# The first strip's third weight group by seven products, with six raw places and a copy pool that opens later

## The chip, the cores and the metric

The kernel runs on one core of a Trainium2 chip. The metric is device time in microseconds. Before the change it was 868.43 us, the median of three runs (868.04 to 869.34).

Five engines work side by side, each through its own list of instructions in order: TensorE (PE) for matmuls, which write to PSUM; VectorE (DVE); ScalarE (ACT); GpSimd (POOL); and SyncE (SP), which here only issues transfers. Semaphores carry the dependences between them.

## The reference

Linear attention for 8 batches of 8 heads, 576 positions and 64 features, followed by a feed-forward block over the 4608 tokens:

```python
kv  = einsum('bhsd,bhse->bhde', k, v)
out = einsum('bhsd,bhde->bhse', q, kv)
x   = out / sqrt(mean(out * out) + 1e-6) * g_norm     # (4608, 512) after the heads are joined
h   = x @ w_in                                        # 512 -> 2048
y   = relu(h) ** 2 @ w_out                            # 2048 -> 512
```

The weights arrive as 64-bit floats and are converted on the chip.

## The kernel before

**Strips.** The 4608 tokens are nine strips of 512. Each strip goes through two products: "up" (x times w_in, with the squared ReLU) and "down" (times w_out). Strip 0 is computed while its weights still arrive. Its up product runs as 16 plain steps (`up_first`, L900 to L918): four groups of the hidden features, four steps in a group, each step eight matmul instructions with 512 columns. After each step ACT makes a ReLU in PSUM (L916) and two squares into the `gt` tiles (L918). Four PSUM places (`fpsum`) take the steps in turn.

From strip 1 on, the up product of a group is made by seven half-size products (`up`, with `ORDER` 1, 2, 6, 5, 7, 3, 4). They use three PSUM banks: 1, 6, 7 and 4 add up in one, 5 and 3 in another, 2 has its own. After 1, 6 and 5 ACT copies the bank as a snapshot (`combine`, L880), and later products are added to these. Seven products need four sums of x (`sums_x`) and three sums of the weights (`sums_in`). Strip 0's down product uses the same scheme with weights (`down`).

**Conversion of weights.** A raw weight comes in pieces of 512 KB. Two pieces make a pair, and a pair has one place in `raw_pool` (five places). For each pair ACT makes two copies (L260 into `w_c`, which has two places, and L262 in place), POOL clamps (L282), and DVE joins the bits in two steps (L284, L288). `convert(n)` emits conversions up to the n-th behind the steps of the up product; the list `PACE` says how far after each. When it emits the conversion of pair n it first emits ACT's copies of pair n+1, and then the loads of later pieces (`load_more`), up to `AHEAD` = 10 pieces ahead. Pairs 0 to 7 are w_in; 8 to 15 are w_out. The last four pairs are also summed by DVE in `sums_out` into tiles called `wt`, which take places of `raw_pool` too, and are stored to DRAM from there (L336).

**Order.** All instructions are emitted by hand in one order, and each engine keeps that order. Between the steps `attend` emits the next pieces of the attention: transposes of q (`t_ps`, copied by ACT at L422), key-value products (`kv_ps`, copied by ACT at L453 and L454 into `kv_all`), products with the queries (`x_ps`, L484, which read `kv_all`), squares (L493), means, and scaled rows. SP issues all loads and stores, in order, too.

**Pools.** SBUF is given out as a stack of pools. The pools for the conversion (`xt_pool`, `raw_pool`, `spare_pool`, `wtmp`) lie on top of it; when strip 0's up product is emitted they are closed, and `stream_pool` and `sum_pool` are opened in the same room. A place there may be written only after the work on what lay there has ended. Both are opened with `reuse_waits="tile"`. The pool of snapshots and outputs (`c_pool`, six places) is opened at the start, below the conversion pools, and has its room to itself.

```python
conv = ExitStack()
xt_pool = conv.enter_context(tc.tile_pool(name="xt", bufs=1))
raw_pool = conv.enter_context(tc.tile_pool(name="raw", bufs=5))
...
conv.close()
stream_pool = ctx.enter_context(tc.tile_pool(name="stream", bufs=6, reuse_waits="tile"))
sum_pool = ctx.enter_context(tc.tile_pool(name="sum", bufs=8, reuse_waits="tile"))
```

Of the kernel before, what the change touches and what calls it, by code (L numbers as in the profile page):

```python
# [10 lines left out]
FP32 = mybir.dt.float32  # L11
# [3 lines left out]
AF = mybir.ActivationFunctionType  # L15
ALU = mybir.AluOpType
# [4 lines left out]
def kernel(  # L21
# [34 lines left out]
    nc = tc.nc  # L56
    P = 128
# [13 lines left out]
    TH = STRIP // 2  # L71
# [4 lines left out]
    SQ = 32  # L76
    Q_ON_PE = 2
    BEHIND = 1.6
    X_ON_PE = 2
    EPS = 1e-6  # L80
    AHEAD = 10
    PACE = (3, 4, 4, 5, 6, 7, 8, 9, 10, 11, 12, 13, 13, 14, 15, 16)
    const = ctx.enter_context(tc.tile_pool(name="const", bufs=1))
    wpool = ctx.enter_context(tc.tile_pool(name="wpool", bufs=1))
# [4 lines left out]
    small = ctx.enter_context(tc.tile_pool(name="small", bufs=3))  # L89
    g_pool = ctx.enter_context(tc.tile_pool(name="g", bufs=4))  # L90
    dram = ctx.enter_context(tc.tile_pool(name="dram", bufs=1, space=bass.MemoryType.DRAM))
    c_pool = ctx.enter_context(tc.tile_pool(name="c", bufs=6))
    conv = ExitStack()
    xt_pool = conv.enter_context(tc.tile_pool(name="xt", bufs=1))
    raw_pool = conv.enter_context(tc.tile_pool(name="raw", bufs=5))
    spare_pool = conv.enter_context(tc.tile_pool(name="spare", bufs=1))
    wtmp = conv.enter_context(tc.tile_pool(name="wtmp", bufs=2))
    psums = ExitStack()
    fpsum = psums.enter_context(tc.tile_pool(name="fpsum", bufs=4, space=bass.MemoryType.PSUM))
# [61 lines left out]
    def load_rest(b, eng):  # L161
        h = b % 2 * (b > Q_ON_PE + 1)
        half = slice(REST * h, REST * (h + 1))
        for t, src in ((k_rest[half], k), (v_rest[half], v)):
            eng.dma_start(out=t, in_=src[b, :, C * P : S].rearrange("h s d -> s h d"))
# [20 lines left out]
    def load_next(q_eng=nc.sync, names="kvq"):  # L186
        u = next(to_load, None)
        if u is not None:
            load(*u, q_eng, names)
# [27 lines left out]
    KH, FH, DH = NP // 2, d_ff // 2, d_model // 2  # L217
    FQ = FC // 2
    WN = 512
    NG = FQ // 2  # L220
# [3 lines left out]
    block = lambda b: w_in[:, :, :, b] if b < 4 else w_s[:, :, :, b - 4]  # L224
# [14 lines left out]
    raw = []  # L239
    raw_pairs = []  # L240

    def load_piece():
        i = len(raw)
        if i < len(sources):
            if i % 2 == 0:
                raw_pairs.append(raw_pool.tile([P, 2, 2, WN // 2], I64, name="raw", tag="raw"))
            t = raw_pairs[i // 2][:, i % 2]
            nc.sync.dma_start(out=t, in_=sources[i])
            raw.append(t)
# [42 lines left out]
    def convert_pair(n, dest):  # L292

        for i in range(acted[0], min(n + 2, len(sources) // 2)):
            convert_pair_on_act(i)
            acted[0] = i + 1
        deque(conversion(pair_words.pop(n), dest, nc.gpsimd), 0)
        load_more(2 * n + 2)

    def load_more(end):  # L300

        while len(raw) < min(end + AHEAD, max(len(sources) - 4, end + AHEAD - 4), len(sources)):
            load_piece()

    def minus(eng, out, a, b):
        eng.tensor_tensor(out=out, in0=a, in1=b, op=ALU.subtract)  # L306
# [3 lines left out]
    def pieces_in(i):  # L310
        g, k = divmod(i // 2, KH)
        convert_pair(i // 2, w_in[:, k, g].rearrange("p (a b) e -> p a (b e)", a=2))

    def sums_in(g):

        nc.scalar.activation(w_in[:, :, g, 0:4], w_in[:, :, g, 0:4], AF.Copy, scale=g_col)
        a11, a21, a12, a22, s1, s2, s4 = (block(b)[:, :, g] for b in range(7))
        nc.vector.tensor_tensor(out=s1, in0=a21, in1=a22, op=ALU.add)
        minus(nc.vector, s2, s1, a11)
        minus(nc.vector, s4, a12, s2)  # L320
        minus(nc.vector, a21, a11, a21)
# [24 lines left out]
    def convert(n):  # L346
        while converted[0] < min(n, len(conversions)):
            fn, a = conversions[converted[0]]
            fn(a)
            converted[0] += 1  # L350
# [337 lines left out]
    xc = {}  # L688

    def halves(s, kh, th):  # L690
        return xt[s][:, ts(th, TH // SQ), ts(kh, KH), :]

    def sums_x(s):
        xc[s] = t1, t2, t3, t4 = [
            sum_pool.tile([P, TH // SQ, KH, SQ], FP32, name=f"x_t{i}", tag="sum") for i in range(4)
        ]
        x = lambda kh, th: halves(s, kh, th)
        minus(nc.vector, t1, x(0, 1), x(0, 0))
        minus(nc.vector, t2, x(1, 1), t1)
        minus(nc.vector, t3, x(1, 1), x(0, 1))  # L700
        minus(nc.vector, t4, x(1, 0), t2)
# [99 lines left out]
    def attend_between(slot, begun, goal, late, first, last):  # L801
# [6 lines left out]
        while slice_at[0] < most:  # L808
# [6 lines left out]
            if fn != send_x:  # L815
                left = sum(f != send_x for f, _ in slices[slice_at[0] : goal])
                if used and (on in used or fn in (root, inverse) or used & {root, inverse}):
                    return
                if left <= last - slot and behind[on] + cost > BEHIND:
                    return  # L820
# [28 lines left out]
    ORDER = (1, 2, 6, 5, 7, 3, 4)  # L849
    BANK = {1: "A", 6: "A", 7: "A", 4: "A", 5: "B", 3: "B", 2: "C"}  # L850
    A_IN = {1: 0, 2: 2, 3: 6, 4: 3, 5: 4, 6: 5, 7: 1}
    B_OUT = {1: 0, 2: 1, 5: 2, 7: 3, 3: 4, 6: 5, 4: 6}
    bank, snap, gq, w_blk = {}, {}, {}, {}

    def open_bank(p):
        b = BANK[p]
        if p in (1, 5, 2):
            bank[b] = fpsum.tile([P, 2, 2 * P], FP32, name=f"ps_{b}", tag="f")
        return bank[b]
# [7 lines left out]
    def product(p, i, lhsT, rhs, n):  # L867

        for k in range(n):
            nc.tensor.matmul(  # L870
                bank[BANK[p]][:, i, :], lhsT=lhsT(k), rhs=rhs(k),
                start=p in (1, 5, 2) and i == 0 and k == 0, stop=k == n - 1, skip_group_check=True,
            )

    def combine(p, c11, c12, c21, c22):

        b = bank[BANK[p]]
        if p in (1, 6, 5):
            snap[p] = c_pool.tile([P, 2, 2 * P], FP32, name=f"snap{p}", tag="c")
            nc.scalar.copy(snap[p], b)  # L880
        elif p == 4:
            c21(b)
        else:
            other, c = {2: (1, c11), 7: (5, c22), 3: (6, c12)}[p]
            c(b, snap[other])

    def quarters(s, g):

        if (s, 11) not in gq:
            for q in (11, 12, 21, 22):  # L890
                gq[s, q] = g_pool.tile([P, FQ, TH], FP32, name="gt", tag="gt")
        return {q: gq[s, q][:, 2 * g : 2 * g + 2, :] for q in (11, 12, 21, 22)}
# [27 lines left out]
    def up(s, g, p):  # L920
        open_bank(p)
        rhs = {
            1: halves(s, 0, 0), 2: halves(s, 1, 0), 3: halves(s, 1, 1),
            4: xc[s][3], 5: xc[s][0], 6: xc[s][1], 7: xc[s][2],
        }[p]
        for i in range(2):
            product(p, i, lambda kc: block(A_IN[p])[:, kc, g, ts(i, P)], lambda kc: rhs[:, :, kc, :], KH)
        dest = quarters(s, g)

        def relu_squared(q):  # L930
            def f(b, a):
                o = dest[q]
                nc.vector.tensor_tensor(out=o, in0=b, in1=a, op=ALU.add)
                nc.vector.scalar_tensor_tensor(out=o, in0=o, scalar=0.0, in1=o, op0=ALU.max, op1=ALU.mult)
            return f

        def last(b):
            nc.scalar.activation(dest[21], b, AF.Relu)
            nc.scalar.activation(dest[21], dest[21], AF.Square)

        combine(p, relu_squared(11), relu_squared(12), last, relu_squared(22))
# [66 lines left out]
    def down(s, p, i):  # L1008
# [27 lines left out]
        def store(th, eh):  # L1036
# [7 lines left out]
            return f  # L1044

        combine(p, store(0, 0), store(0, 1), store(1, 0), store(1, 1))


# [310 lines left out]
    for s in range(N_STRIP):  # L1359
# [7 lines left out]
        if s >= DEEP_UP:  # L1367
            steps = [(0.5, up_slot, (s, slot)) for slot in range(55)]
        elif s == 0:
            steps = [(2, up_first, (g, fh, i)) for g in range(NG) for fh in range(2) for i in range(2)]  # L1370
        else:
            steps = [(1, up, (s, g, p)) for g in range(NG) for p in ORDER]
        n_up = len(steps)
# [9 lines left out]
                goal = min(pair_ends, key=lambda end: abs(end - goal))  # L1383
        total, done = sum(w for w, _, _ in steps), 0
        for i, (w, fn, a) in enumerate(steps):
            if s == 0 and i < n_up:

                if i == 0:
                    load_next()
                    load_rest(1, nc.sync)  # L1390
                    load_next()
                if i == 1:
                    load_next()
                if i == 2:
                    for b in range(2):
                        load_q_rest(b, nc.sync)
                if i == 14:
                    for b in range(2):
                        store_first(b)
            elif s == 0 and i == n_up:  # L1400
                convert(len(conversions))
                conv.close()

                stream_pool = ctx.enter_context(tc.tile_pool(name="stream", bufs=6, reuse_waits="tile"))
                sum_pool = ctx.enter_context(tc.tile_pool(name="sum", bufs=8, reuse_waits="tile"))
            if s == 0 and n_up <= i < n_up + 2:
# [5 lines left out]
            fn(*a)  # L1412
            if s == 0 and i < n_up:

                convert(PACE[i])
            done += w
            if s:
                clock[0] += 3.2 if i >= n_up else 2.2 if s == DEEP else 1.2
                soon = tiles_due and tiles_due[0][2][0] // NT == s + 1
                if i == n_up + 10:  # L1420
                    while tiles_due and tiles_due[0][2][0] // NT == s + 1:
                        _, f, a = tiles_due.popleft()
# [35 lines left out]
                sums_in((7, 8, 9, 12).index(i - n_up))  # L1458
            if i == n_up + 11:
                sums_x(1)  # L1460
            n = i + 1 - (n_up - 6)
            pairs, m = divmod(max(n - 2 * NP, 0), 3)
            attend(min(ready[0] + min(max(n, 0), 2 * NP) + (n >= 2 * NP) + 4 * pairs + (0, 2, 2)[m], goal))
            while deep_due and i not in (n_up + 1, n_up + 4, n_up + 12, n_up + 13):
# [38 lines left out]
```

## Time and profile before

| what | value |
|---|---|
| median of three runs | 868.43 us |
| the profiled execution | 868.8 us, of which the span of its instructions is 867.0 |
| PE busy | 857.8 us, 99% of the span |
| DVE busy | 702.0 us, 81% |
| ACT busy | 348.9 us, 40% |
| POOL busy | 328.1 us, 38% |
| strip 0's up steps on PE | up to 82.3 us |
| strip 0's down product on PE | from 83.1 to 138.2 us |

Times in the profile are counted from the start of the span. A row of a timeline gives the start, the duration, the engine, the line of the kernel, the operation, the tiles it writes and reads, its shape, and how many instructions are merged; in brackets stands the idle time before it and what ended that. Matmuls overlap, so the time that one takes on the engine is the distance to the next one's start, not its duration. A row of the lines' view gives minimum, median and maximum duration in ns. Shares of busy time are means over stages with different limits.

### The profile page before, as it was taken

To read this page: it belongs to the slowest core of one execution; us is meant where nothing else is said; L and a number is where in the kernel's file an instruction comes from. 1 tells how busy PE (TensorE), PEld (TensorE's weight loads), DVE (VectorE), ACT (ScalarE), POOL (GpSimd) and SP (SyncE) were. 2 spreads that over 40 slices of the span, in tenths; PEclk is the share of its full clock that TensorE was granted. 3 is DMA by queue.
4 is the path that set the end of the run, shared out by engine and by line. 5 is a ranking of instruction groups with operands and counts; after the bars stand their busy time and mean duration, and the time that the engine had idled before them with its cause. 6 is when DMAs were issued, how large, how long until landed. Compare 5 with 4: busy or idle time off the path is not lost.

```text
span 867.0 us, 32426 instructions
## 1 busy us (share of the span) xinstructions
PE 857.8 (99%) x14176; PEld 804.2 (93%) x14176; DVE 702.0 (81%) x1132; ACT 348.9 (40%) x777; POOL 328.1 (38%) x335
## 2 busy tenths in 40 slices
PE   7999999999999999999999999999999999999998
PEld 6445888889999999999999999999999999999998
DVE  3768988879877996789688967897889777975887
ACT  4888241320048303750356034901491148102810
POOL 1223004630458223730574045704470447145700
PEclk9999999999999999999999999999999999999999
DMA  9898998999999997989698979987678856885583
GB/s 307 277 362 269 274 377 239 295 332 353 280 264 259 342 325 233 228 307 344 209 244 273 341 239 281 283 297 270 198 236 302 301 165 221 293 282 196 175 315 121
DMA packets 169469, 236.46 MB, mean 273 GB/s; under 512 B 78704, under 2 KB 133744, under 8 KB 161008
## 3 DMA queue, kind: packets, MB, share of 16 engines
q1 hardware_dynamic: 169024, 234.33, 83.5%
q8 instruction: 111, 1.82, 0.9%
q14 instruction: 30, 0.25, 0.1%
q10 hardware_dynamic: 304, 0.07, 0.0%
HBM read 197.66 MB, written 36.70 MB: 270 GB/s over the span
## 4 chain that ended last, share of the span: by engine, by line
PE 83%; DMA 7%; DVE 5%; ACT 3%; SPq 1%; issue 1%; DVEq 0%; ACTq 0%
PE ps_A L865 36%; PE ps_B L865 31%; PE ps_C L865 5%; PE ps_A L870 4%; DMA raw<-in_moe_w_in_dram 2%; PE kv_ps L448 2%; PE x_ps L484 2%; PE ps_B L870 2%; DVE w_t L306 1%; DMA w_deep<-w_t 1%; DMA raw<-in_moe_w_out_dram 1%; DMA w_blk<-w_deep 1%; PE ps_C L870 1%; DMA first_qkv<-in_v_dram 1%; ACT w_c L260 1%
## 5 line engine op out<-in xcount | busy, mean ns | idle before, releaser
L865 PE MATMUL ps_B<-w_blk,g_s 128*64 128x128 f32 x2016 | 122.0, 273 | 0.0
L865 PEld LDWEIGHTS ps_B<-w_blk,g_s 128*64 128x64 f32 x2016 | 112.6, 137 | 0.1
L306 POOL TENSOR_TENSOR x_l<-xT 128x256 f32<-128x256 f32 x21 | 16.2, 773 | 230.2 <-PE ps_A L865 230.2
L865 PE MATMUL ps_B<-w_blk,gt 128*64 128x128 f32 x1504 | 94.1, 273 | 0.3 <-DMA w_blk<-w_deep 0.3
L865 PE MATMUL ps_A<-w_blk,g_s 128*64 128x128 f32 x1536 | 92.2, 273 | 0.0
L1323 POOL TENSOR_TENSOR snap<-snap,gt 128x512 f32<-128x512 f32 x35 | 46.2, 1320 | 112.5 <-ACT snap L1328 93.6
L865 PEld LDWEIGHTS ps_A<-w_blk,g_s 128*64 128x64 f32 x1536 | 85.7, 137 | 0.0
L865 PEld LDWEIGHTS ps_B<-w_blk,gt 128*64 128x64 f32 x1504 | 84.6, 137 | 0.8 <-PE ps_B L865 0.5
L1328 ACT COPY snap<-ps_A 128x512 f32<-128x512 f32 x63 | 36.8, 585 | 103.6 <-PE ps_A L865 96.2
L1263 ACT ACTIVATE gt<-gt 128x512 f32<-128x512 f32 x112 | 70.2, 627 | 9.9 <-DVE gt L1323 9.9
L1264 ACT ACTIVATE gt<-gt 128x512 f32<-128x512 f32 x112 | 70.7, 631 | 3.5
L865 PE MATMUL ps_A<-w_blk,gt 128*64 128x128 f32 x1152 | 71.2, 273 | 0.0
L865 PEld LDWEIGHTS ps_A<-w_blk,gt 128*64 128x64 f32 x1152 | 64.7, 137 | 0.0
L1112 ACT COPY o_sb<-ps_A 128x128 f32<-128x128 f32 x24 | 6.4, 265 | 144.7 <-PE ps_A L865 109.4
L306 DVE TENSOR_TENSOR gt<-gt 128x2048 f32<-128x2048 f32 (+1 forms) x29 | 59.7, 2063 | 0.0
L1111 DVE TENSOR_TENSOR o_sb<-o_sb,ps_B 128x256 f32<-128x256 f32 (+1 forms) x123 | 47.4, 386 | 14.3 <-ACT o_sb L1112 9.5
L865 PE MATMUL ps_A<-x_l,w_in 128*64 128x128 f32 x896 | 58.6, 273 | 0.2 <-DVE gt L1323 0.2
L1323 POOL TENSOR_TENSOR gt<-gt,snap 128x512 f32<-128x512 f32 x42 | 52.5, 1279 | 15.1 <-DVE snap L1323 15.1
L865 PEld LDWEIGHTS ps_A<-x_l,w_in 128*64 128x64 f32 x896 | 50.8, 137 | 0.5 <-DVE gt L1323 0.5
L865 PE MATMUL ps_B<-x_l,w_blk 128*64 128x128 f32 x784 | 51.2, 273 | 0.0
L865 PE MATMUL ps_A<-x_l,w_blk 128*64 128x128 f32 x784 | 51.2, 273 | 0.0
L1112 ACT COPY o_sb<-ps_B 128x128 f32<-128x128 f32 x31 | 8.2, 265 | 96.3 <-PE ps_B L865 96.3
(214 smaller groups left out, 1900.2 us busy)
## 6 DMA issues: line engine op xcount, KB each, us to landing
w_blk<-w_deep SPq DMA_DIRECT2D x56, 1024.0 KB, 7.3
w_blk<-w_out SPq DMA_DIRECT2D x56, 768.0 KB, 6.2
w_blk<-w_in_deep SPq DMA_DIRECT2D x49, 768.0 KB, 5.8
raw<-in_moe_w_in_dram SPq DMA_DIRECT2D x16, 512.0 KB, 9.2
raw<-in_moe_w_out_dram SPq DMA_DIRECT2D x16, 512.0 KB, 8.0
k<-in_k_dram SPq DMA_DIRECT2D x29, 256.0 KB, 4.9
v<-in_v_dram SPq DMA_DIRECT2D x29, 256.0 KB, 5.2
x_d<-x_q SPq DMA_DIRECT2D x27, 256.0 KB, 4.8
```

Source lines behind the costliest of these rows:

```text
L260: nc.scalar.activation(c, high_f, AF.Copy, scale=EXPONENT)
L306: eng.tensor_tensor(out=out, in0=a, in1=b, op=ALU.subtract)
L448: nc.tensor.matmul(ps[ts(h, D), i], lhsT=a, rhs=w, start=i == 0 and c == 0, stop=c == C, skip_group_check=True)
L484: nc.tensor.matmul(ps[half, r, i, ts(p, D)], lhsT=q[row, half], rhs=kvd[b, p][row, row], start=True, stop=True)
L865: nc.tensor.matmul(ps[half], lhsT=lhsT[:, half], rhs=rhs, start=start, stop=stop, skip_group_check=True)
L870: nc.tensor.matmul(bank[BANK[p]][:, i, :], lhsT=lhsT(k), rhs=rhs(k), start=p in (1, 5, 2) and i == 0 and k == 0, stop=k == n - 1, skip_gro ...
L1111: add = lambda out, a, b: nc.vector.tensor_tensor(out=out, in0=a, in1=b, op=ALU.add)
L1112: yield nc.scalar.copy(q[:, 3:4], small(1))
L1263: nc.scalar.activation(o, o, AF.Relu)
L1264: nc.scalar.activation(o, o, AF.Square)
L1323: add = lambda eng, out, a, b: eng.tensor_tensor(out=out, in0=a, in1=b, op=ALU.add)
L1328: nc.scalar.copy(t, ps)
```

## The change

Group 2 of strip 0's up product (`HALVED = 2`) is made by seven products with `up`, in place of four plain steps. Strip 0 has therefore 19 up steps. What belongs to it:

- The list `TURN` maps the new steps to the old turns, so conversions of group 2 are emitted behind the steps 9, 11, 13 and 14 of the list, which are products 2, 5, 3 and 4. The first product has none of its own.
- The sums of strip 0's x are written into the `gt` places of group 3 behind step 3, and the weights' sums (`first_sums_in`) into those of group 2 behind step 5. Both are on DVE.
- The additions of a quarter are on DVE; the squared ReLU of one of them (12) is on ACT.
- The later weight sums of group 2 for the other strips (`sums_in`) take three DVE instructions instead of four.
- The raw pool has six places instead of five, and `AHEAD` is 12 instead of 10.
- `c_pool` is opened after the conversion pools are closed, ahead of `stream_pool`. Until then a pool of its own, `snap_pool` with three places, takes the snapshots of group 2; it belongs to the conversion pools.

```diff
+    HALVED = 2
+    TURN = (*range(8), 7, 8, 8, 9, 9, 10, 11, *range(12, 16))
-    AHEAD = 10
+    AHEAD = 12
-    c_pool = ctx.enter_context(tc.tile_pool(name="c", bufs=6))
-    raw_pool = conv.enter_context(tc.tile_pool(name="raw", bufs=5))
+    raw_pool = conv.enter_context(tc.tile_pool(name="raw", bufs=6))
+    snap_pool = conv.enter_context(tc.tile_pool(name="snap", bufs=3))
...
+    def first_sums_in(g):
+        a11, a21, a12, a22 = (block(b)[:, :, g] for b in range(4))
+        dest = quarters(0, g)
+        first_w[:] = s1, s2, s4 = [dest[q] for q in (22, 12, 21)]
+        nc.vector.tensor_tensor(out=s1, in0=a21, in1=a22, op=ALU.add)
+        minus(nc.vector, s2, s1, a11)
+        minus(nc.vector, s4, a12, s2)
+        minus(nc.vector, a21, a11, a21)
...
     def sums_in(g):
+        if g == HALVED:
+            minus(nc.vector, s2, a22, a21)
+            nc.vector.tensor_tensor(out=s1, in0=s2, in1=a11, op=ALU.add)
+            minus(nc.vector, s4, a12, s2)
+            return
...
     def sums_x(s):
+        else:
+            free = quarters(0, HALVED + 1)
+            ts_x = [
+                free[q].rearrange("p i t -> p (i t)").rearrange("p (a k t) -> p a k t", k=KH, t=SQ) for q in free
+            ]
...
         if p in (1, 6, 5):
-            snap[p] = c_pool.tile([P, 2, 2 * P], FP32, name=f"snap{p}", tag="c")
+            pool, tag = (snap_pool, "snap") if snap_pool else (c_pool, "c")
+            snap[p] = pool.tile([P, 2, 2 * P], FP32, name=f"snap{p}", tag=tag)
...
+            w = first_w[b - 4] if s == 0 and b > 3 else block(b)[:, :, g]
...
+                if s == 0 and q == 12:
+                    nc.scalar.activation(o, o, AF.Relu)
+                    nc.scalar.activation(o, o, AF.Square)
+                    return
...
+                if g == HALVED:
+                    steps += [(1, up, (s, g, p)) for p in ORDER]
...
             elif s == 0 and i == n_up:
                 convert(len(conversions))
                 conv.close()
+                snap_pool = None
+                c_pool = ctx.enter_context(tc.tile_pool(name="c", bufs=6))
                 stream_pool = ctx.enter_context(tc.tile_pool(name="stream", bufs=6, reuse_waits="tile"))
...
-                convert(PACE[i])
+                if i == 3:
+                    sums_x(0)
+                if i == 5:
+                    first_sums_in(HALVED)
+                convert(PACE[turn])
```

## The prediction, made before the change was run

> **What bounds the kernel now.** I read the page first, then TensorE's timeline over the first strip, then ScalarE's and the DMA queue's over the same stretch, then the list of waits.
>
> The page's first part (engine, busy us and share of the span):
>
> ```profile
> PE 857.8 (99%) x14176; PEld 804.2 (93%) x14176; DVE 702.0 (81%) x1132; ACT 348.9 (40%) x777; POOL 328.1 (38%) x335
> ```
>
> PE has no slack, so PE work removed is time gained, unless PE is made to wait. PE's timeline (start us, us, instructions):
>
> ```profile
> 51.08 3.60 PE L911 MATMUL ps_A<-xT,w_in 128*128 128x512 f32 x8
> ...
> 91.34 1.16 PE L484 MATMUL x_ps<-kv_all,qT 64*64 64x64 f32 x64
> 92.43 3.72 PE L870 MATMUL ps_C<-w_s,gt 128*128 128x256 f32 x16
> ...
> 138.25 1.89 PE L870 MATMUL ps_A<-xT,w_in 128*128 128x256 f32 x8
> 139.98 1.89 PE L870 MATMUL ps_C<-xT,w_in 128*128 128x256 f32 x8
> ```
>
> The third group starts at 51.08. A full step of it takes 3.43 us (51.08 to the next step's 54.51); a product of the seven, as strip 1 has them, 1.73 us (138.25 to 139.98). ScalarE's timeline in that stretch:
>
> ```profile
> 53.38 1.14 ACT L260 ACTIVATE w_c<-raw 128x1024 f32<-128x1024 f32 x1 [1.60 <-DVE w_in L288]
> 54.42 1.15 ACT L262 ACTIVATE raw<-raw 128x1024 int32<-128x1024 uint32 x1
> 55.47 0.59 ACT L916 ACTIVATE ps_C<-ps_C 128x512 f32<-128x512 f32 x1
> 56.09 0.66 ACT L918 ACTIVATE gt<-ps_C 128x256 f32<-128x256 f32 x2
> 57.53 1.16 ACT L260 ACTIVATE w_c<-raw 128x1024 f32<-128x1024 f32 x1 [0.78 <-DMA raw<-in_moe_w_out_dram]
> ...
> 90.71 0.59 ACT L880 COPY snap<-ps_A 128x512 f32<-128x512 f32 x1 [2.87 <-PE ps_A L870]
> 91.45 0.20 ACT L453 COPY kv_all<-kv_ps 64x64 f32<-64x64 f32 x1 [0.16 <-PE kv_ps L448]
> ```
>
> ACT takes the last step of group 1 at 55.47, though PE ended it at 51.1: it is 4.4 us behind, which costs nothing now, as four PSUM places lie between them. At 90.71 it copies the first snapshot of the second product (the L880 row) as soon as PE is done. The stores of the second weight sums, in the queue's timeline and their line's view:
>
> ```profile
> 88.75 8.14 SPq L336 DMA_DIRECT2D w_out<-wt  x8
> 100.71 0.81 SPq L965 DMA_DIRECT2D w_blk<-w_out  x2
> ```
>
> ```profile
> L336 SPq DMA_DIRECT2D w_out<-wt x4: 508/630/701, 94.3 to 96.2; - x4
> ...
> DMA to landing us min/median/max: 4.1/4.3/4.4
> ```
>
> The last is issued at 96.2 and lands 4.4 us later, at 100.6. Keep that number.
>
> **The change part by part.**
>
> *Products.* Removed: four steps of 3.43 us, 13.74. Added: seven products of 1.73 us, 12.12. PE saves 1.62 us.
>
> *ScalarE in the group.* Removed: four times a ReLU and two squares, 1.16 us each to the next row, 4.6. Added: three snapshots of 0.59 and twice a ReLU and a square at 0.6 each (512 columns as in the L916 row), 4.2. Little changes in sum, but the order does. The third product (6) writes the bank that the first (1) left, so PE must wait for the first snapshot, which ACT reaches only behind group 1's last step and the two conversion copies emitted after it (1.05 us each). The 1.60 us before 53.38 is put down to VectorE, but the pair's second piece was issued at 45.85 and landed 7.4 us later, at 53.3: it is a load, and the sixth place brings it 2.5 to 3 us earlier. So ACT reaches the last step at about 54 (instead of 55.47), leaves it at 55.2, ends the copies at 57.5 to 58 and the snapshot at 58.1 to 58.6. PE has finished products 1 and 2 at 54.5 and waits about 3.6 to 4.1. The next pair of copies stands before snapshot 6, and its weights land at 59.9 now; product 7 may wait up to another 0.7, product 4 about 0.4 for VectorE's addition, queued behind a conversion. The group loses 3.6 to 5.2, saves 1.62, and ends 2.0 to 3.5 us later than now.
>
> *VectorE.* Added: four sums of x and four of the weights at 0.65, three additions with PSUM and two ReLU-squares at 0.68, 8.6 us. The list of waits has 15.2 us in which it waits for POOL's clamps between 33 and 90; that covers them. One sum fewer in the later weight sums (0.65) is off the path.
>
> A two-input VectorE sum that started under a running clamp took 1.41 us instead of 0.69 (72.61). Among the new sums that adds perhaps twice 0.7; the clamp's own wait gap covers it, but through the two places of w_c it can reach ACT at about 52 and lengthen the group's wait by up to 0.7. The Trainium skill's "SBUF — State Buffer" (Who interferes with whom) has the same as an exclusive lock: whichever of the two starts later waits for the other's end. By it any of the eight sums could wait a whole clamp; the sum above stays within its bounds.
>
> *Loads.* A sixth raw place and 12 pieces ahead put two pieces (1.3 us each on the queues) before batch 1's ten loads on SP. Batch 1 is first used at 61.38 and has landed by 36.3: 2.5 us of delay is covered by 25. Pieces after it come about as now, the third w_out pair bound by bandwidth. No DMA is added or lost; POOL issues none.
>
> *Room.* The second product's copy pool was opened at the start; now it is opened after the conversion pools close, in their room. Its 12 KB cover the 8 KB of xT and the first 4 KB of the raw pool. The stream and sum pools opened beside it carry reuse_waits="tile"; this one doesn't. What that form gives shows now: the POOL row "L1449 MEMSET xT", in the stream pool's first place, ran at 82.57, while stores from the raw pool were out until 100.6. Opened plainly, I take a pool's first use to wait for everything in the pools whose room it takes, so for all of the raw pool. That includes the sums' places and their last store. The bounds: no wait at all (only xT lies under the first place, free when PE ends the strip), or all of it, until 100.6. I take all, since the keyword would have nothing to do otherwise.
>
> The first use is the L880 copy. It now runs at 90.71. It would start at about 100.7 (the sums' end moves by perhaps 0.2 by VectorE's added work, and SP is issue-bound there) and end at 101.3. Queued behind it on ACT: the two kv_all copies, 0.4, to 101.7. Behind those PE's L484 needs the last quarter of its matmuls, 0.3, with the hand-overs to 102.1. Now that row ends at 92.43: +9.7 us. PE's own lateness from the group vanishes in this wait, as does the saving: both lie ahead of an end that a store sets. PE would stand still for some 6 to 7.5 us.
>
> *After a standstill.* At the start of the trace, after PE's idle 1.36 us and what lay before it:
>
> ```profile
> 1.36 3.22 PE L392 MATMUL t_ps<-ident 128*128 128x128 f32 x14 [1.36 <-POOL ident masks.py:199]
> 4.51 1.09 PE L420 MATMUL t_ps<-ident,q 128*64 128x128 f32 x16
> ...
> 24.74 0.60 PE L624 MATMUL xt_ps<-ident,x_n 128*128 128x128 f32 x4
> ```
>
> 14 matmuls of 128x128 take 3.15 us, 0.225 each; at 24.74 four take 0.44 (to the next row's 25.18), 0.11 each. Fourteen at that pace are 1.54, so a slow start cost 1.6 us, although the granted clock reads 1.00 throughout. After the 1.41 us gap at 15.00 nothing of this shows. Between these, 0 and 1.6, I take 1.6: a standstill of 6 us is nearer to a start from rest.
>
> The Trainium skill's "TensorE: Matmul & The Clock Gate" (What's actually happening) says the array falls to half rate after an idle window of about 3.4 us and needs about as long a busy one to return. By it the price is 1.7 us, an estimate, and the group's own wait of up to 4 us might start it too.
>
> *Further on.* PE waits 0.46 us at 131.24 for VectorE's o_sb. VectorE is later by about 8 (its first means follow the squares behind L484), less than PE, so that gap closes: -0.46. The first features of strip 1 now need the xT place over the last stores, free at 100.7; they come at 103.97 plus the delay.
>
> **Sum.** 9.7 + 1.6 - 0.46 = +10.8 us. The profiled execution took 868.8 (span 867.0 and 1.8 around it) and would take 879.6; it is 0.37 above the median of the runs, 868.43, so I forecast 879.3.
>
> **The rivals.**
> 1. *The wait comes, PE returns at full rate.* For it: the 15.00 gap. +9.2: 877.7.
> 2. *The copy pool waits only for what lies under its place.* Then group 2 decides: +2.0 to +3.5 less 0.46, 870 to 871.5, centre 871.0; its wait of 3.6 could bring the slow start too.
> 3. *Not slower: only the saving counts.* ACT would have to end the first snapshot by 54.5, 3.6 us before the order of its queue lets it, and the store must bind nothing. -1.62: 866.8. Against it: ACT's row at 55.47. It decides where the snapshot's lateness falls under the 1.62 saved.
>
> **How the numbers follow.** A difference under 0.2% (1.7 us) can't be told from no change in this kernel. Forecast 0.60; rival 1 0.17; rival 2 0.12 (a third of it within 0.2%); rival 3 0.08 (half within, half beyond, by what else shifts); 0.03 for sums and stores that end still later. Faster 0.04, same 0.04 + 0.04 = 0.08, slower 0.88. The range from 871.0 leaves out rival 3 and half of rival 2, and reaches 881.5: the forecast with the store 1.5 later and a slow start somewhat longer.
>
> **What would show it.** Right: in the profile after, L880's first copy in the second product is released by the DMA w_out<-wt near 101, PE idles before L484 for 6 us or more, and matmuls behind it are twice as far apart for some 3 us. In group 2, PE waits about 4 us for a snapshot. Wrong: that copy runs within 1 us of PE's end at about 93, or ACT is less than 2 us behind at group 2's start.

## The result, and the profile after

The changed kernel takes 883.62 us (median of five runs, 883.02 to 886.18) beside 869.13 us for the kernel before (868.04 to 871.50): a ratio of 1.0169, interval 1.0149 to 1.0190. It is slower, as predicted, but by 14.5 us instead of 10.8. The measured time lies 2.1 us above the top of the predicted range.

In the kernel after, the lines have moved: the snapshot copy is L905 (before L880), the small products L894 (L870), `x_ps` L503 (L484), ACT's first conversion copy L262 (L260), the copies of `kv_all` L472 and L473, the stores of `wt` L355 (L336), the plain up steps L936 (L911).

From the page of the kernel after, the busy times and the row of the granted clock (40 slices of 22.1 us):

```profile
PE 862.1 (98%) x14200; PEld 813.1 (92%) x14200; DVE 713.3 (81%) x1144; ACT 348.3 (39%) x772; POOL 330.7 (37%) x335
...
PEclk9999799999999999999999999999999999999999
```

PE does less work than before but counts 4 us more as busy, and the fifth slice (88 to 110 us) shows a lower clock. PE's timeline after:

```profile
49.64 1.89 PE L894 MATMUL ps_A<-xT,w_in 128*128 128x256 f32 x8
51.36 1.89 PE L894 MATMUL ps_C<-xT,w_in 128*128 128x256 f32 x8
58.32 3.42 PE L894 MATMUL ps_A<-gt 128*128 128x256 f32 x8 [5.06 <-ACT snap L905]
...
102.51 0.93 PE L503 MATMUL x_ps<-kv_all,qT 64*64 64x64 f32 x16 [7.09 <-ACT kv_all L472]
103.37 6.50 PE L894 MATMUL ps_C<-w_s,gt 128*128 128x256 f32 x16
109.70 0.60 PE L447 MATMUL tr_ps<-ident,q_rest 128*128 128x128 f32 x4
```

Both waits that the prediction named are there: 5.06 us in the third group, for the first snapshot, and 7.09 us ahead of the last quarter of `x_ps`. The sixteen products after the second wait take 6.33 us (103.37 to 109.70); before they took 3.56 (from 92.43 to the next row). ACT's timeline after shows who holds them:

```profile
52.25 1.17 ACT L262 ACTIVATE w_c<-raw 128x1024 f32<-128x1024 f32 x1 [2.48 <-DVE w_in L290]
...
54.35 0.67 ACT L941 ACTIVATE ps_C<-ps_C 128x512 f32<-128x512 f32 x1
...
57.64 0.63 ACT L905 COPY snap<-ps_A 128x512 f32<-128x512 f32 x1
...
61.77 0.59 ACT L905 COPY snap<-ps_A 128x512 f32<-128x512 f32 x1 [1.44 <-PE ps_A L894]
63.50 0.59 ACT L905 COPY snap<-ps_B 128x512 f32<-128x512 f32 x1 [1.14 <-PE ps_B L894]
63.98 1.16 ACT L262 ACTIVATE w_c<-raw 128x1024 f32<-128x1024 f32 x1
...
67.68 0.63 ACT L962 ACTIVATE gt<-gt 128x512 f32<-128x512 f32 x1 [1.47 <-DVE gt L960]
...
101.77 0.59 ACT L905 COPY snap<-ps_A 128x512 f32<-128x512 f32 x1 [10.77 <-DMA w_out<-wt]
102.25 0.20 ACT L472 COPY kv_all<-kv_ps 64x64 f32<-64x64 f32 x1
```

The row at 101.77 is the wait that the prediction named: the first use of the late copy pool, released by the DMA of the weight sums. The windows after give the busy share of PE and, behind the bracket, the clock that it was granted:

```profile
54.00:58.00 4.00, 0.00 (x0) 0.98 1.03 358
58.00:61.25 3.25, 2.93 (x7) 0.50 1.06 409
61.25:62.00 0.75, 0.75 (x4) 1.00 1.03 401
...
99.00:102.00 3.00, 0.00 (x0) 0.50 0.52 155
102.00:106.00 4.00, 3.49 (x22) 0.50 0.78 283
106.00:109.00 3.00, 3.00 (x8) 0.50 0.78 328
109.00:110.00 1.00, 1.00 (x7) 0.99 0.00 0
```

After each of the two waits PE runs at half its clock (0.50). The kernel before reads 1.00 in all windows from 40 to 120 us.

**Where the time went.** Nearly all of it went in the first strip. The table takes, from PE's timeline of each kernel, the start of the third group, the start of strip 1's first product, and the time between, called the stage below; each row is one execution. From strip 1's start to the end of PE's last product it takes 725 to 729 us in these seven traces, without an order that follows the change (726.0 before, 728.9 after, 728.2 in e10, which is no slower than before). The two gaps that the trace after has there (1.21 us at 548.20, 1.60 at 554.12) were absent when the same kernel ran again, and are taken as scatter.

| kernel | third group starts | strip 1 starts | between |
|---|---|---|---|
| before | 51.08 | 138.25 | 87.17 |
| before, again (e9) | 49.82 | 136.86 | 87.04 |
| after | 49.64 | 151.24 | 101.60 |
| after, again (e4) | 49.39 | 150.22 | 100.83 |
| after, keyword on the copy pool (e1) | 49.66 | 142.15 | 92.49 |
| after, third group plain (e2) | 49.96 | 147.37 | 97.41 |
| after, both (e10) | 49.52 | 135.45 | 85.93 |

The stage grew by 14.4 us (101.60 less 87.17), close to the difference of the medians: 14.5 here, 13.1 when the changed kernel ran again (e4).

### The profile page after: what moved, and what is told of

The parts are those of the page before. It is cut to its first block, busy times and chain, and to the rows that moved or that the text cites. A ratio compares the mean times of both kernels' runs of the same rounds, so it can differ in the third digit from the quotient of the medians.

```text
span 883.0 us, 32490 instructions
## 1 busy us (share of the span) xinstructions
PE 862.1 (98%) x14200; PEld 813.1 (92%) x14200; DVE 713.3 (81%) x1144; ACT 348.3 (39%) x772; POOL 330.7 (37%) x335
## 4 chain that ended last, share of the span: by engine, by line
PE 86%; DMA 6%; DVE 3%; ACT 3%; SPq 1%; issue 1%; POOL 0%; DVEq 0%; ACTq 0%
PE ps_A L889 35%; PE ps_B L889 31%; PE ps_A L894 6%; PE ps_C L889 5%; PE ps_B L894 4%; DMA raw<-in_moe_w_in_dram 2%; PE x_ps L503 2%; PE ps_C L894 2%; PE kv_ps L467 2%; DMA v<-in_v_dram 1%; DMA q<-in_q_dram 1%; DMA more_qkv<-in_q_dram 1%; DVE wt L308 1%; ACT w_c L262 1%; DVE w_c L286 1%
## 5 line engine op out<-in xcount | busy, mean ns | idle before, releaser
L889 PE MATMUL ps_A<-x_l,w_s 128*64 128x128 f32 x672 | 44.2, 273 | 2.2 <-issue 1.6
```

The source lines that it names most:

```text
L889: nc.tensor.matmul(ps[half], lhsT=lhsT[:, half], rhs=rhs, start=start, stop=stop, skip_group_check=True)
```

## The experiments

Each kernel is the changed one with the edit shown, unless it says otherwise. They ran in three batches beside the kernel before, whose medians there were 870.12 (19 runs: e1 to e4), 869.49 (29 runs: e5 to e8) and 870.47 (17 runs: e9 and e10).

### e1: the copy pool with the keyword

```diff
-                c_pool = ctx.enter_context(tc.tile_pool(name="c", bufs=6))
+                c_pool = ctx.enter_context(tc.tile_pool(name="c", bufs=6, reuse_waits="tile"))
```

> The changed kernel (883.6 us) with one keyword more: the copy pool is opened with reuse_waits="tile", as the two pools beside it. Theory A, the plain pool waits for the whole raw pool: the first snapshot of the second product runs within 1 us of PE's end of that product, the 7.09 us wait before L503 goes, and with it the half-speed stretch behind it (+2.8 us); what is left is the third group's loss, about 3.2 us at the end of the first product less 0.5 found back later: about 871.8. Rival B, what lies under the first place is itself late (or the stores hold ACT in another way): the wait stays, about 883.

Measured: 873.03 us (871.80 to 875.43, 12 runs), ratio 1.0024 (1.0005 to 1.0044). ACT's timeline of this kernel at the snapshot:

```profile
95.34 0.58 ACT L905 COPY snap<-ps_A 128x512 f32<-128x512 f32 x1 [2.87 <-PE ps_A L894]
```

And PE's timeline of it, at the third group and at `x_ps`:

```profile
58.28 3.78 PE L894 MATMUL ps_A<-gt 128*128 128x256 f32 x8 [5.00 <-ACT snap L905]
61.85 3.09 PE L894 MATMUL ps_B<-gt 128*128 128x256 f32 x8
...
95.97 1.16 PE L503 MATMUL x_ps<-kv_all,qT 64*64 64x64 f32 x64
97.06 3.72 PE L894 MATMUL ps_C<-w_s,gt 128*128 128x256 f32 x16
```

The snapshot is released by PE, the `x_ps` row is whole again, and the sixteen products run at full speed. One keyword takes away 9.1 us of the stage (101.60 to 92.49) and 10.2 us of the median (from 883.19, the changed kernel in the same batch, e4). What stays is the group's wait, 5.00 us, and the half clock behind it: products 6 and 5 take 3.57 and 2.93 us from start to start instead of 1.73.

### e2: the third group plain, the pool as in the change

```diff
-    HALVED = 2
-    TURN = (*range(8), 7, 8, 8, 9, 9, 10, 11, *range(12, 16))
+    HALVED = 9
+    TURN = tuple(range(16))
...
-                if i == 3:
-                    sums_x(0)
-                if i == 5:
-                    first_sums_in(HALVED)
```

> The changed kernel with the third group in its four plain steps again and no sums for it; the six raw places, the 12 pieces ahead and the late copy pool stay. Theory A, the wait for the stores hides whatever PE does before it: PE arrives 3 to 5 us earlier, waits 10 to 12 us in place of 7.1, and the time stays within 1 us of 883.6. Rival C, the two losses add up: the group's loss of 3.2 to 5 us comes back, 878.5 to 880.5.

Measured: 878.82 us (876.72 to 884.23, 6 runs), ratio 1.0100 (1.0064 to 1.0136). PE's timeline of this kernel:

```profile
98.81 0.93 PE L503 MATMUL x_ps<-kv_all,qT 64*64 64x64 f32 x16 [8.18 <-ACT kv_all L472]
99.67 6.33 PE L894 MATMUL ps_C<-w_s,gt 128*128 128x256 f32 x16
105.84 0.60 PE L447 MATMUL tr_ps<-ident,q_rest 128*128 128x128 f32 x4
```

The pool alone makes PE wait longer, since PE arrives earlier; yet the kernel is 4 us faster than the changed one. The expectation by theory A, within 1 us of 883.6, failed; the time lies in rival C's range, but not by rival C's way. PE's own lateness from the group is taken up by the wait, as theory A has it. But the store that ends the wait is itself later with the group: it releases ACT at 98.07 here and at 101.77 in the changed kernel. The two timelines of ACT show why. These are its conversion copies here, in the stretch where the changed kernel has its group:

```profile
57.77 1.16 ACT L262 ACTIVATE w_c<-raw 128x1024 f32<-128x1024 f32 x1 [0.41 <-DMA raw<-in_moe_w_out_dram]
...
61.03 1.15 ACT L262 ACTIVATE w_c<-raw 128x1024 f32<-128x1024 f32 x1
...
64.30 1.17 ACT L262 ACTIVATE w_c<-raw 128x1024 f32<-128x1024 f32 x1
```

With plain steps ACT is behind PE and waits for no product: in this stretch it waits only for two loads (0.95 us at 54.00, 0.41 at 57.77). With the seven products it stands in the queue for product 6 (1.44), for product 5 (1.14) and for VectorE's addition (1.47), 4.05 us in the rows shown above, and the conversion copies stand behind those waits. POOL's clamps of the two kernels, counted from the start, are level at 47.6 us, up to 2.6 apart until 59, then 3.0 (65.22 against 62.27) and 4.6 (70.12 against 65.55). That last pair is the one that counts. VectorE's timeline of the changed kernel:

```profile
66.95 0.69 DVE L960 TENSOR_TENSOR gt<-ps_B,snap 128x512 f32<-128x512 f32 x1
...
71.20 1.23 DVE L286 SCALAR_TENSOR_TENSOR w_c<-w_c,raw 128x1024 int32<-128x1024 int32 x1 [1.17 <-POOL w_c L284]
```

And the same join (the second row above) in e2:

```profile
66.92 1.23 DVE L286 SCALAR_TENSOR_TENSOR w_c<-w_c,raw 128x1024 int32<-128x1024 int32 x1 [0.94 <-POOL w_c L284]
```

VectorE's addition at 66.95 comes right behind product 7 (PE's row at 65.03, 1.89 us). ACT's squared ReLU at 67.68 waits for the addition, and the copy at 68.88, the clamp at 70.12 and the join at 71.20 follow one another. From this join on VectorE works without a gap to the last sum, in both kernels, and the last store lands 30.5 us after the join (31.1 in e2). The clamps after it, up to 4.8 us later than e2's, hold nothing.

### e3 and e8: PE kept busy through the wait

```diff
+        if (b, ps_of[0]) == (1, 3):
+            keep_busy(ps[:, 0], 55)
```

`keep_busy` is a helper of the kernel that multiplies the identity by itself; the key-value product behind it overwrites the result. e3 has the 55 products shown (110 instructions), e8 has 27.

> The changed kernel with 55 matmuls by the identity (128x64, about 6 us) put ahead of the key-value product before the wait, so that PE stands still for about 1 us and not 7. Theory D, PE's half speed after 102.5 comes of its standstill: the sixteen matmuls that took 6.3 us take about 3.5, and the time falls by 2.5 to 2.8 us, to about 881. Rival E, they were slow for another reason (weights, transfers): the stretch and the time stay, 883.6.

> The changed kernel (plain copy pool) with 27 matmuls by the identity ahead of the key-value product before the wait. In the run before, 55 of them took 12.4 us, so that they ended 4 us after the wait, but the sixteen matmuls behind it took 3.56 us instead of 6.3. 27 should take 6.1 and leave PE idle for about 1 us. Theory D, half speed comes of standing still: 2.5 to 2.8 us less than the changed kernel, 880.5 to 881. Rival E: no gain, 883.2.

e3 took 887.64 us (883.69 to 891.18, 4 runs), ratio 1.0190 (1.0147 to 1.0232). PE's timeline of e3, whose lines are two further on:

```profile
93.78 12.39 PE L411 MATMUL kv_ps<-ident 128*128 128x64 f32 x110
...
106.83 1.16 PE L505 MATMUL x_ps<-kv_all,qT 64*64 64x64 f32 x64
107.92 3.72 PE L896 MATMUL ps_C<-w_s,gt 128*128 128x256 f32 x16
111.48 0.60 PE L447 MATMUL tr_ps<-ident,q_rest 128*128 128x128 f32 x4
```

As a time it is a miss: the filling lasted 12.3 us, some 4 beyond the wait. But sixteen products after a stretch without standstill take 3.56 us, and the clock reads 1.00 there; so the 6.33 us go with the standstill. Against the transfers as the cause e3 says little, since few were left by then (85 GB/s during the sixteen products, beside 318 in the changed kernel). The kernel before settles that: its sixteen products take the same 3.56 us beside 331 GB/s.

e8 took 885.59 us (883.55 to 888.45, 4 runs), ratio 1.0165 (1.0118 to 1.0212). PE stood for only 1.76 us, but its windows show the clock falling all the same:

```profile
102.00:104.00 2.00, 0.35 (x24) 1.00 0.35 102
104.00:104.50 0.50, 0.39 (x6) 0.86 1.69 197
104.50:107.50 3.00, 3.00 (x20) 0.50 0.75 317
107.50:108.00 0.50, 0.50 (x3) 0.72 1.10 459
```

The half clock begins when PE has been back for 0.3 us, and the sixteen products take 4.93 us. Here the expectation of full speed failed, and the time lies above both forecasts (880.5 to 881 and 883.2). The 1.4 us that the sixteen products save are lost again: ACT is released only at 103.37 here, 1.6 us later than in the changed kernel, and the stage is 101.98.

### e4: the changed kernel again

> The changed kernel once more, for a second trace. In the first one PE falls behind by another 1.4 us at 548 us (a wait for a load of q) and 1.9 us at 554 us (no releaser shown). If that belongs to the change, both are there again and the lateness against the kernel before grows from about 12.5 us to about 16; if it is scatter of one execution, it stays between 12.5 and 14. Time 883 to 884.5 either way.

Measured: 883.19 us (882.65 to 885.33, 4 runs), ratio 1.0144 (1.0108 to 1.0181). Group wait 4.97, `x_ps` wait 6.67, sixteen products 5.27 instead of 6.33 us. The time is as expected, and at PE's end the kernel is 13.8 us later than the first trace of the kernel before, inside the 12.5 to 14 that were given for scatter (15.9 in the first trace of the changed kernel). The stage repeats within 0.8 us; the length of the half clock doesn't (below).

### e5, e6, e7: what holds the first snapshot

All three have e1's keyword. e5 emits VectorE's sums of the weights two steps later; e6 emits the conversions from step 7 on two steps later; e7 does both.

```diff
-                if i == 5:
+                if i == 7:
                     first_sums_in(HALVED)
```

```diff
-    TURN = (*range(8), 7, 8, 8, 9, 9, 10, 11, *range(12, 16))
+    TURN = (*range(7), 6, 6, 7, 7, 8, 8, 9, 10, *range(12, 16))
```

> The run before with the tile-wise copy pool (873.0, 2.9 above its kernel before), and the four weight sums of the third group emitted behind step 7 instead of step 5. Theory F, the group's wait is a chain: the sums hold VectorE, this holds the free place of w_c, that holds ScalarE for 2.46 us at 52.29, and the first snapshot is behind it. Then ScalarE's 2.46 us wait goes, PE's wait for the snapshot falls from 5.0 to about 2.6 us and perhaps too short for the half-speed stretch behind it (1.5 to 3 us): 868.5 to 870.5. Rival G, ScalarE is late by the loads or by its own work alone: wait 4.5 to 5, time 873.

> The tile-wise copy pool, the sums behind step 5 as in the change, and the conversions from that of step 7 on each emitted two steps later, so that no conversion copy stands between the last plain step and the first snapshot on ScalarE. Theory F: ScalarE still waits 2.46 us, but saves the 2.07 us of copies ahead of the snapshot: PE's wait falls from 5.0 to about 2.9. Time 869 to 871. Rival H, what is moved behind comes back: later products or the second sums wait for the conversions, and the time stays at 872 to 873.

> Both together: the sums behind step 7 and the conversions two steps later, with the tile-wise copy pool. Theory F: the two parts add up, the first snapshot is done about 0.5 us after PE's second product, no half-speed stretch, and the group is 1 to 1.2 us shorter than four plain steps; time 0.5 to 1.5 us under the kernel before. Rival H: VectorE, late with the sums or the conversions, takes the gain back at 131 us (its o_sb addition): within 0.5 us of the kernel before, or above.

| kernel | us (range, 12 runs each) | ratio | PE's wait for product 6 | stage |
|---|---|---|---|---|
| e1 | 873.03 (871.80 to 875.43) | 1.0024 (1.0005 to 1.0044) | 5.00, ACT | 92.49 |
| e5 | 872.79 (869.82 to 880.60) | 1.0029 (1.0000 to 1.0058) | 2.98, ACT | 90.41 |
| e6 | 874.02 (870.67 to 879.65) | 1.0045 (1.0016 to 1.0074) | 2.90, ACT | 92.26 |
| e7 | 873.73 (871.17 to 878.56) | 1.0044 (1.0017 to 1.0070) | 1.26, DVE | 90.67 |

The wait for product 6 falls as expected in e5 and e6 (2.6 and 2.9 us were forecast): in e5 ACT's 2.48 us stop at 52.25 is gone (its copy starts at 49.65 without a wait), so that stop was VectorE's sums ahead of the join that frees `w_c`. But the medians can't be told apart from e1's, so the times that theory F forecast (868.5 to 870.5, 869 to 871, and below the kernel before) failed in all three. PE's timeline of e7 shows what took the place:

```profile
54.72 1.97 PE L894 MATMUL ps_A<-gt 128*128 128x256 f32 x8 [1.26 <-DVE gt L308]
...
62.79 1.99 PE L894 MATMUL ps_A<-gt,w_in 128*128 128x256 f32 x8 [0.92 <-DVE gt L960]
...
71.37 0.66 PE L436 MATMUL t_ps<-ident,q 128*128 128x128 f32 x4 [1.98 <-ACT qT L441]
```

The sums that were moved out of ACT's way are now late for PE itself, the additions after them, and the postponed conversions stand ahead of the copy of qT. e7 has no half clock in the group, but it has one behind the last of these waits: the clock reads 0.50 from 72.07 to 75.49, and the plain step at 71.86 takes 5.23 us instead of 3.53. The three waits (4.2 us) and the 1.7 of this step, less the 1.62 saved, are 4.2 of the 4.7 us by which e7's stage exceeds that of the plain group (e10, 85.93). In none of the four orders tried does the group gain: its work on VectorE and ACT holds up the conversions, or they hold it up.

### e9 and e10: the kernel before again, and the sixth place alone

e10 is e2's edit and e1's keyword together: a plain third group, six raw places, loads twelve pieces ahead, the copy pool late.

> The kernel before once more, for a second trace of it. In the first one the third group started at 51.08; in all kernels with six raw places it started between 48.9 and 50.0. If that is scatter of the opening (gaps of 1.41 and 0.82 behind loads at 15.00 and 17.21), the group starts here at 49.0 to 50.5 and the second product's x_ps row ends 0.5 to 2 earlier than 92.43. If the sixth place brings it, the group starts at 50.8 to 51.4 again. In both cases TensorE's granted clock reads 1.00 from 40 to 120.

> The third group plain again, six raw places, the copy pool opened late with reuse_waits="tile". Theory: what is left of the loss beside the pool's wait is the group's own wait and its half-speed stretch. Then this kernel has no wait above 1 us before its second product, the granted clock reads 1.00 from 40 to 120, the last store of the sums lands at about 98, and the time is that of before, ratio 0.998 to 1.001 (867.5 to 870.5 beside a before of 869.5). Rival: the sixth place with two pieces more ahead, or the later pool, costs on its own what the kernel with the tile keyword alone still lost, 0.24%: ratio 1.002 or more, 871.5 or more, and the extra time shows as loads of batch 1 landing late or as new waits behind them.

e9: one run of 866.6 us. Its third group starts at 49.82, so the 1.4 us by which the changed kernels started it earlier than the first profile are scatter of the opening, not the sixth place. Its stage is 87.04 us, the same as in the first trace.

e10: 868.48 us (866.47 to 871.25, 12 runs), ratio 0.9980 (0.9964 to 0.9996). PE's timeline of e10:

```profile
89.26 1.16 PE L503 MATMUL x_ps<-kv_all,qT 64*64 64x64 f32 x64
90.36 3.72 PE L894 MATMUL ps_C<-w_s,gt 128*128 128x256 f32 x16
...
128.54 7.07 PE L894 MATMUL ps_A<-w_blk,gt 128*128 128x256 f32 x32
```

No wait is left: the last row is the place where the kernel before waits 0.46 us for `o_sb`. The stage is 1.2 us shorter than before, and the interval lies just under 1; this is the only variant here whose median lies below that of the kernel before. Its gain, a fifth of a per cent, is at the limit below which the prediction counts a difference as none. The theory that the group makes e1's remaining loss holds, and the rival (the sixth place or the later pool costs it) falls.

## Why the prediction was right in kind and 3.7 us short

**Right: the mechanism that decides.** The plainly opened pool waits for the whole raw pool, its last store included, with ACT's copies of `kv_all` queued behind. e1 shows it by one keyword. Rival 2, a pool that waits only for what lies under its place, was priced at 871.0 us, 2.6 above the median that the prediction went by; e1, where the snapshot no longer waits for the store, lies 2.9 above the kernel before of its batch. That these two agree is partly luck: the price left out the half clock, and e1's stage is 5.3 us longer than before (92.49 against 87.17), so that the median's 2.9 and the one trace's 5.3 don't match, which stays open.

**Right in kind: the group.** PE waits for the first snapshot, which stands behind ACT's last step and two conversion copies. The wait was 5.06 us instead of 3.6 to 4.1, since ACT stopped 2.48 us at 52.25 for the place of `w_c`; the prediction had up to 0.7 for that. With the half clock the group costs 6.6 us of the stage (e1's 92.49 less e10's 85.93): 5.00 of wait, 2.98 for the 5.97 us that PE ran at half clock (58.28 to 64.25), less the 1.62 saved, 6.4.

**Wrong: "the sums' end moves by perhaps 0.2".** This is the step that failed. Counted from the third group's start, the last store landed 49.5 us later in the kernel before (100.6) and 52.1 later after (101.7). VectorE's join that decides it moved by 2.55 us (from 70.09 less 51.08 to 71.20 less 49.64). The `x_ps` row's end moved from 41.35 to 53.73 after that start, by 12.4 us and not 9.7. The prediction looked at VectorE, found its 8.6 us covered by waits for POOL, and stopped there. That covering held: from the join to the last landing it takes 30.5 us in both kernels. The delay comes through ACT, of which the prediction said that little changes in sum but the order does; it followed the order to PE's wait and not on to the conversions, which now stand behind products that are late by that same wait. e2 gives the size without the other parts: ACT is released 48.1 us after the third group's start there and 52.1 in the changed kernel, 4.0 more (3.7 counted from the start of the trace). The net is smaller than 4.0 because in e2 the store is 1.4 earlier than in the kernel before; the six places and the earlier loads are the likely reason, and no run tests them alone.

**Wrong in size: the slow restart.** Predicted 1.6 us, measured 2.77 in the changed kernel (6.33 less 3.56) and 1.71 when it ran again. The group's wait, of which the prediction said that it might start it too, did start it, in all traces with a wait of 2.9 us or more there; in the kernel as changed it lies ahead of the later wait, whose end a store sets.

**Right: the gap that closes.** No wait for `o_sb` is left in the kernel after, as the -0.46 had it.

The corrected sum is 12.4 + 2.8 - 0.5 = 14.7 us, against 14.4 in the stage and 14.5 in the medians. The claim that PE's lateness and the saving both vanish in the wait holds for PE's own time, but not for the group as a whole. The group alone costs 6.6 us and the pool alone 11.5 (e2's 97.41 less 85.93), together 18.0, and measured were 15.7 (101.60 less 85.93). The 4.2 us between e2 and the changed kernel are the store's 4.0 and 0.16 of longer half clock.

## What to carry to other kernels

A pool that is opened late in used room takes over the waits of everything that lay there; look at the first instruction that uses it, and at what stands behind that one in its engine's queue. When an engine that used to run behind is given work that reads another engine's newest result, everything else in its queue inherits that wait, so follow its queue to the end of the stage, and not only to the next wait. And a standstill of the tensor engine can cost more than its length: here waits of about 2 us or more brought 1.5 to 3.3 us of half clock on top.

## What the runs showed of the hardware

**The half clock comes in pieces of 3.41 us.** Adding up the granted clock in windows of a quarter of a microsecond, the half clock lasted 3.41 us (group, after), 3.41 (e5), 3.41 (e6), 3.42 (e3's group), 3.41 (e7, 72.1), 3.42 (e8, 104.4), 6.83 (e1), 6.83 (e8's group), 6.83 twice in e4, 10.24 (second wait, after) and 10.24 (e2): one, two or three times the same length. It began between 0.8 us after PE was back (e6: at 56.17, PE back at 55.41) and 4.1 us before (e2: at 94.74, PE back at 98.81). In the three traces with two such stretches, their starts lie 40.96 us (after: 57.82 and 98.78), 44.37 (e4: 55.72 and 100.09) and 47.79 (e8: 56.58 and 104.36) apart, which is 12, 13 and 14 times 3.413. So within a trace the pieces lie on one grid, whatever the waits between them, and what a standstill costs depends on where in that grid it falls: the sixteen products took 6.33 us in one run of the changed kernel and 5.27 in another. The Trainium skill's "TensorE: Matmul & The Clock Gate" (What's actually happening) says that the activity is judged in windows of 3413 ns that run freely and don't start anew with the kernel; these lengths and distances agree with it.

**Short waits are enough.** PE idle for 2.90 us (e6) and 2.98 us (e5) brought a full piece of half clock, and so did 1.98 us in e7 and 1.76 us in e8, both behind small products; 1.26 us in e7 and 1.62 us in e6 (at 72.23) did not. The idle stretch of about 3.4 us that the prediction reckoned with is therefore not needed here. What share of a piece must be idle wasn't measured.

**VectorE beside POOL.** Of the four new sums of the weights, two took about twice their time. VectorE's timeline after:

```profile
45.52 1.41 DVE L323 TENSOR_TENSOR gt<-w_in 128x512 f32<-128x512 f32 x1
46.96 0.69 DVE L308 TENSOR_TENSOR gt<-gt,w_in 128x512 f32<-128x512 f32 x1
47.69 1.53 DVE L308 TENSOR_TENSOR gt<-w_in,gt 128x512 f32<-128x512 f32 x1
49.14 0.68 DVE L308 TENSOR_TENSOR w_in<-w_in 128x512 f32<-128x512 f32 x1
```

POOL's clamps ran from 44.38 to 46.39 and from 47.63 to 48.67. The prediction had two such collisions at 0.7 us each; measured are 0.72 and 0.84.
